# K/Q transposes and score masks of a recurrent attention step, issued as four 32-column TensorE tiles each

## The chip, the cores and the metric

The kernel runs on one core of a Trainium2 chip. The metric is the device time of one launch in microseconds, the median of several runs. A core has a matrix engine (TensorE, PE in the profile; its weight loads are listed apart as PEld), three engines for elementwise work (VectorE or DVE, ScalarE or ACT, GpSimd or POOL), and SyncE (SP), which issues most transfers. TensorE multiplies a stationary operand, loaded with a weight load, by a moving operand that is streamed through, and writes into PSUM, from where VectorE or ScalarE copies the result to SBUF. A weight operand of 32 columns can be given a place in the array, a tile of 32 of its 128 columns, named in the code by `tile_position=(0, 32*j)`; its result then lies in 32 of the 128 partitions of PSUM.

## What is computed

Four layers, A, B, A, B, each with a layer norm before it and a residual sum after it, over 2048 tokens of width 640. The change lies in layer B, a recurrence over 64 segments of 32 tokens with 8 rows of memory:

```python
def _B_ref(x, mem0, Wq, Wk, Wv, Wo, seg_len):
    B, S, Dm = x.shape
    H, Dh = (Wq.shape[1], Wq.shape[2])          # 32, 128
    M = mem0.shape[1]                           # 8
    scale = Dh ** (-0.5)
    n_seg = S // seg_len                        # 64
    L = M + seg_len                             # 40
    idx = jnp.arange(L)
    mask = (idx[:, None] < M) | (idx[:, None] >= idx[None, :])
    mem = mem0
    outs = []
    for s in range(n_seg):
        xs = x[:, s * seg_len:(s + 1) * seg_len, :].copy()
        h = jnp.concatenate([mem, xs], axis=1)
        q = jnp.einsum('btd,dhe->bhte', h, Wq)
        k = jnp.einsum('btd,dhe->bhte', h, Wk)
        v = jnp.einsum('btd,dhe->bhte', h, Wv)
        scores = jnp.einsum('bhqe,bhke->bhqk', q, k) * scale
        scores = jnp.where(mask[None, None], scores, -1000000000.0)
        p = _softmax(scores, axis=-1)
        o = jnp.einsum('bhqk,bhke->bhqe', p, v)
        o = jnp.einsum('bhte,hed->btd', o, Wo)
        mem = o[:, :M, :].copy()
        outs.append(o[:, M:, :])
    return jnp.concatenate(outs, axis=1)
```

The memory rows of one segment are outputs of the segment before it, so the 64 segments of a layer run one after another. Two layers B make 128 steps.

## The kernel before

`layer_B` runs a Python loop over the steps (line 854), which writes out one instruction stream per engine. The wrapper `_OrdNC` (line 115) ties each instruction of an engine to the one before it, so every engine runs its instructions in the order of the code; all of them carry line 105 in the profile, and they are told apart by the names of their tiles.

A step works on 32 columns: the 8 memory rows that the step before has just produced and the 24 token rows of the segment after (the last 8 token rows of each segment, the tails, are projected ahead in batches, and arrive through DRAM as `b_tl` for keys and queries and as `b_Vth` for values). In order:

- `thin_mm` (line 658) makes the projections Ka, Qa, Kb, Qb (lines 944 to 950), heads 0 to 15 in the a halves and 16 to 31 in the b halves. Each is 20 products of 128x32 weights (the columns `b_HX`) with 512 moving columns, in four tiles of 32 columns. Each result is copied to a tile `b_kq` by ScalarE (Ka, Kb, Qb) or VectorE (Qa).
- `transp4` (line 667) transposes each copy, with 4 transposes of 128x128, into PSUM: TPak, TPaq, TPbk, TPbq (lines 953 to 963). The copy is the stationary operand, the identity `C.identb` the moving one. TPbq has a PSUM tile of its own (tag "tail").
- After each, VectorE copies the 8 memory rows to `b_KT` or `b_QT` of this step (`scatter`, line 674), and ScalarE the 24 token rows to those of the next step (`x_scatter`, line 867).
- `mask_mm` (line 878) opens the score tiles SP0 (8 groups of 40 columns) and SP1 (4 groups) with the mask: one product of the identity with 320 columns of `mask12`, and one with 160. The first stands ahead of TPbq, the second behind it.
- `scores` (line 885) adds the products of queries and keys in tiles of 32 columns: 16 of heads 0 to 15 (`b_QT`), then 32 small ones with the tails' queries (`b_QZ`), all into SP0, then 16 of heads 16 to 31 into SP1. SP0 is thus complete after 48 of the 64.
- Softmax (lines 968 to 979): maximum over SP0, then over SP1, subtraction, exponential on ScalarE, sum, reciprocal, and the probabilities `b_Pm` and `b_Px`. Meanwhile TensorE makes the values Va and Vb (lines 983 and 985, in tiles as above), a part of the batch projections of tails (`tail_unit`, in 110 of the steps), and in some steps the transposes of the next layer-normed input (`ln_spread`, tile `b_lntps`).
- `p_transp` transposes the probabilities (PTP), `pv` multiplies them by the values (OTP), `o_mm` applies the output weights (OPS), and lines 1028 to 1043 bring the 8 new memory rows into the columns of the next step (`b_msb`, `b_MT`, `b_HX`), with which Ka of the next step begins.

The PSUM tiles of the pool "b_ps" (5 buffers) are taken in turn; SP1 follows Qb in its buffer, and Va follows TPak. What an engine waits for is settled by semaphores. One is raised at the last transpose of a set, one at the last of the 48 products into SP0, and one at the last of the 16 into SP1.

Of the kernel before, what the change touches and what calls it, by code (L numbers as in the profile page):

```python
# [542 lines left out]
def layer_B(nc, tc, C, W, x_src, xb_src, x_dst, mem0, B_Wv, B_Wo, nsteps=64, out_bf16=False, tag=""):  # L543
    SCB = 1.0 / math.sqrt(128.0)
    nc_raw = nc
    nc = _OrdNC(tc, nc_raw, engines=ORDER_ENGINES)
# [4 lines left out]
    with ExitStack() as ctx:  # L551
# [21 lines left out]
        def ps_tile(shape, dtype, name):  # L573
            return pp.tile(shape, dtype, name=name, tag="ps")
# [4 lines left out]
        mask12 = st.tile([128, 12, 40], BF16, name="b_mask12")  # L579
# [87 lines left out]
        def transp4(sb, name, tp=None):  # L667
            if tp is None:
                tp = ps_tile([128, 4, 128], BF16, name)
            for i in range(4):  # L670
                nc.tensor.transpose(tp[:, i, :], sb[:, 128 * i:128 * i + 128], C.identb[:])
            return tp

        def scatter(eng, tp, b, dst_t, t0, t1, c0):
# [107 lines left out]
        for nm, b in jobs:  # L782
            ps = thin_mm(cols, W.wk if nm == "K" else W.wq, b, f"b_{nm}p")
            sb = kqp.tile([128, 512], BF16, name="b_kq", tag="kq")
# [5 lines left out]
        for (nm, b), sb in zip(jobs, sbs):  # L790
            tp = transp4(sb, "b_TP")
            scatter("dve" if nm == "K" else "act", tp, b, KT[0] if nm == "K" else QT[0], 8, 32, 8 if nm == "K" else 0)
# [61 lines left out]
        for s in range(nsteps):  # L854
# [23 lines left out]
            def mask_mm(a):  # L878
                g0, g1 = GR[a]
                SP = ps_tile([128, g1 - g0, 40], F32, f"b_SP{a}")  # L880
                nc.tensor.matmul(SP[:].rearrange("p g k -> p (g k)"), lhsT=C.identb[:], rhs=mask12[:, g0:g1, :].rearrange("p g k -> p (g k)"),
                                 start=True, stop=False, skip_group_check=True)
                return SP

            def scores(SPs):
# [65 lines left out]
            qb = kq(Qb, "act", SCB)  # L951

            TPak = transp4(ka, "b_TPak")
            scatter("dve", TPak, 0, KT[s], 0, 8, 32)
            x_scatter(TPak, 0, KT)
            TPaq = transp4(qa, "b_TPaq")
            scatter("dve", TPaq, 0, QT[s], 0, 8, 24)
            x_scatter(TPaq, 0, QT)
            TPbk = transp4(kb, "b_TPbk")
            scatter("dve", TPbk, 1, KT[s], 0, 8, 32)  # L960
            x_scatter(TPbk, 1, KT)
            SPa = mask_mm(0)
            TPbq = transp4(qb, "b_TPbq", po.tile([128, 4, 128], BF16, name="b_TPbq", tag="tail"))
            scatter("dve", TPbq, 1, QT[s], 0, 8, 24)
            x_scatter(TPbq, 1, QT)
            SPb = mask_mm(1)
            scores((SPa, SPb))
            soft_max(0, SPa)
# [59 lines left out]
            if not last:  # L1028
# [5 lines left out]
                for pi, (ca, cb) in enumerate(parts):  # L1034
                    mt = ps_tile([128, cb - ca, 8], F32, f"b_MT{pi}")
                    for c in range(ca, cb):
                        for q in range(4):
                            o = 64 * c + 32 * (q % 2)
                            nc.tensor.matmul(mt[32 * q:32 * q + 32, c - ca, :], lhsT=msb[:, o:o + 32], rhs=selm[:, q // 2, :],
                                             start=True, stop=True, tile_position=(0, 32 * q), skip_group_check=True)  # L1040
# [107 lines left out]
```

## Time and profile before

| | |
|---|---|
| median of 3 runs | 2867.46 us (2866.17 to 2868.26) |
| the profiled execution | 2871.54 us, its span 2869.8 us |
| granted TensorE clock, mean | 0.975 |
| DMA | 156.40 MB, mean 54 GB/s |
| HBM read, written | 95.65 MB, 51.38 MB |
| layer B's steps in the span | from 461 to 1444 us and from 1880 to 2862 us, about |
| b_Ka, b_Qa, b_Kb, b_Qb, b_Va, b_Vb | 2520 products each, 379 to 381 ns each |
| b_TPak, b_TPaq, b_TPbk, b_TPbq | 512 transposes of 128x128 each, 219 to 222 ns each |
| b_SP<-b_mask | 128 products of 320 columns, 299 ns, and 128 of 160, 233 ns |
| b_SP<-b_KT | 4096 products with b_QT, 186 ns each, 4096 with b_QZ, 181 ns |
| VectorE's copies of the transposes (b_KT, b_QT) | 128 each of 223 to 226 ns |

The duration of a product runs from its start to the modelled end of its way through the array. Products overlap, so what a set costs is read from where the next set starts, not from the sum of the durations. "128*32 128x512" after a product's names is its stationary and its moving operand; "x20" means 20 of them in a row. In the timeline a number in brackets is the time for which the engine stood idle before the instruction, with the tile that it waited for.

### The profile page before, as it was taken

The page shows a single profiled execution, that of the slowest core. Times are in us where ns is not written, and L with a number is a line of the kernel's source. Part 1 is how long each engine was busy: PE and PEld are TensorE (multiplying, and loading weights), DVE is VectorE, ACT ScalarE, POOL GpSimd, SP SyncE. Part 2 cuts the span into 40 slices and gives each one's busy share as a digit, 9 for nine tenths or more (in the row PEclk, how much of TensorE's full clock was granted, in tenths as well). Part 3 has the DMA queues.
Part 4 walks back from the last instruction along what each step waited for, and adds up shares of the span by engine and source line. Part 5 has one row for each costly group of instructions (what it writes and reads, how often), then busy time and mean ns, then how long its engine had stood idle before and what let it go on. Part 6 is the DMA issues. An engine that isn't in the chain of part 4 may idle for free.

```text
span 2869.8 us, 145239 instructions
## 1 busy us (share of the span) xinstructions
PE 2671.2 (93%) x64776; PEld 1669.4 (58%) x64776; DVE 1646.2 (57%) x4428; ACT 1555.7 (54%) x3390; POOL 633.2 (22%) x1506
## 2 busy tenths in 40 slices
PE   5899998999999999999969999889999999999988
PEld 2455555666666666665535555556666666666655
DVE  5778854555555555544468878545555555555544
ACT  3777863545445455544438777544455455445533
POOL 3456551100000000000025666400000000010000
PEclk8999999999999999999989999999999999999999
DMA  5110144222221122111130111621111111111110
GB/s 212 53 43 28 33 142 118 44 43 43 44 43 42 42 46 43 40 40 29 23 120 20 57 47 35 198 71 40 42 39 38 43 41 41 42 39 38 38 22 19
DMA packets 322947, 156.40 MB, mean 54 GB/s; under 512 B 245776, under 2 KB 311056, under 8 KB 319248
## 3 DMA queue, kind: packets, MB, share of 16 engines
q1 hardware_dynamic: 320880, 136.63, 18.8%
q8 instruction: 506, 8.29, 1.2%
q10 hardware_dynamic: 1440, 10.49, 1.0%
q14 instruction: 121, 0.99, 0.1%
HBM read 95.65 MB, written 51.38 MB: 51 GB/s over the span
## 4 chain that ended last, share of the span: by engine, by line
PE 61%; DVE 13%; ACT 4%; DMA 3%; issue 2%; POOL 1%; SPq 0%; ACTq 0%; DVEq 0%; POOLq 0%
PE b_OPS L105 11%; PE b_Ka L105 6%; PE b_Qb L105 5%; PE b_Kb L105 5%; PE b_Qa L105 5%; PE b_SP L105 4%; PE b_OTP L105 3%; PE b_OPSd L105 3%; DVE b_ssum L105 3%; PE b_tail L105 2%; PE b_vtail L105 2%; DVE b_negmax L105 2%; PE b_PTP L105 2%; DVE b_SP L105 2%; ACT b_E L105 2%
## 5 line engine op out<-in xcount | busy, mean ns | idle before, releaser
L105 PEld LDWEIGHTS <-b_HX 128*32 128x32 bf16 x15360 | 412.1, 97 | 374.1 <-issue 16.5
L375 DVE TENSOR_REDUCE a_nm<-a_S 128x2 f32<-128x1024 f32 (+3 forms) x512 | 403.5, 811 | 92.3 <-PE a_T L407 70.8
L410 ACT ACTIVATE a_PT<-a_T 128x1024 bf16<-128x1024 f32 (+1 forms) x384 | 341.0, 892 | 51.9 <-PE a_T L407 46.7
L105 POOL COPY b_OTdef<-b_OTsb 128x256 bf16<-128x256 bf16 x128 | 51.2, 400 | 1360.0 <-DVE b_OTsb L105 1288.6
L105 PE MATMUL b_OPS<-b_wo,b_OTsb 128*32 128x320 bf16 x8192 | 327.0, 311 | 12.7 <-issue 7.6
L105 PEld LDWEIGHTS <-b_OTsb 128*32 128x32 bf16 x8192 | 217.0, 100 | 104.2 <-DVE b_OTsb L105 28.1
L412 POOL TENSOR_SCALAR_AFFINE_SELECT a_PT<-a_PT 128x256 bf16<-128x256 bf16 (+1 forms) x384 | 197.3, 516 | 235.6 <-ACT a_PT L410 234.4
L105 ACT CAST b_msb<-b_OPS 128x128 bf16<-128x128 f32 x252 | 61.5, 295 | 294.2 <-PE b_OPS L105 294.2
L105 DVE CAST b_HX<-b_MT 128x16 bf16<-128x16 f32 x248 | 44.2, 178 | 268.8 <-PE b_MT L105 257.5
L105 ACT CAST b_kq<-b_Kb 128x512 bf16<-128x512 f32 x128 | 74.9, 585 | 201.4 <-PE b_Kb L105 201.4
L105 DVE TENSOR_SCALAR b_kq<-b_Qa 128x512 bf16<-128x512 f32 x128 | 88.5, 692 | 157.3 <-PE b_Qa L105 157.2
L105 DVE CAST b_OTsb<-b_OTP 128x160 bf16<-128x160 f32 (+1 forms) x384 | 122.0, 373 | 90.5 <-PE b_OTP L105 90.4
L105 PE MATMUL b_Ka<-b_wk,b_HX 128*32 128x512 bf16 x2520 | 159.2, 381 | 6.0 <-DVE b_HX L105 0.3
L105 PE MATMUL b_Va<-b_wv,b_HX 128*32 128x512 bf16 x2520 | 161.0, 380 | 0.0
L105 PE MATMUL b_Vb<-b_wv,b_HX 128*32 128x512 bf16 x2520 | 160.3, 379 | 0.0
L407 PE MATMUL a_T<-a_q,a_kT 32*128 32x512 bf16 (+3 forms) x1024 | 139.5, 306 | 21.2 <-DVE a_nm L375 14.6
L105 DVE COPY b_KT<-b_TPak 128x128 bf16<-128x128 bf16 x128 | 28.7, 224 | 227.2 <-PE b_TPak L105 227.2
L105 PE MATMUL b_Qb<-b_wq,b_HX 128*32 128x512 bf16 x2520 | 157.9, 379 | 0.0
L105 PE MATMUL b_Qa<-b_wq,b_HX 128*32 128x512 bf16 x2520 | 157.8, 379 | 0.0
L105 PE MATMUL b_Kb<-b_wk,b_HX 128*32 128x512 bf16 x2520 | 157.8, 379 | 0.0
L105 PEld LDWEIGHTS <-b_kq 128*128 128x128 bf16 x2080 | 116.9, 98 | 69.9 <-ACT b_kq L105 55.6
L105 ACT CAST b_kq<-b_Ka 128x512 bf16<-128x512 f32 x128 | 74.9, 585 | 147.0 <-PE b_Ka L105 147.0
(196 smaller groups left out, 5586.7 us busy)
## 6 DMA issues: line engine op xcount, KB each, us to landing
b_QKd<-b_tu SPq DMA_DIRECT2D x128, 128.0 KB
b_tl<-b_QKd SPq DMA_DIRECT2D x128, 128.0 KB
b_wv<-in_B_Wv_dram SPq DMA_DIRECT2D x10, 1024.0 KB
b_wo<-in_B_Wo_dram SPq DMA_DIRECT2D x16, 640.0 KB
b_VTd<-b_vt SPq DMA_DIRECT2D x256, 32.0 KB
b_Vth<-b_VTd SPq DMA_DIRECT2D x512, 16.0 KB
b_XO<-xres SPq DMA_DIRECT2D x256, 30.0 KB
b_wk<-in_B_Wk_dram ACTq DMA_DIRECT2D x5, 1024.0 KB
```

Of the source, the lines that this page charges most:

```text
L105: r = f(*a, **k)
L375: nc.vector.tensor_reduce(out=nm[:, qc, 2 * pr:2 * pr + 2], in_=X[:, :, o:o + w_], axis=AX.X, op=ALU.max, negate=True)
L407: nc.tensor.matmul(Y[:, e, o:o + w_], lhsT=kT[rows, 128 * kc:128 * kc + 128], rhs=q2[rows, 128 * kc:512], start=True, stop=True, tile_posi ...
L410: nc.scalar.activation(out=PT[:, :, b:b + width], in_=Y[:, :, 0:width], func=ACT.Exp, scale=SC)
L412: nc.gpsimd.affine_select(out=dv, in_=dv, pattern=[[0, 2], [0, diag], [1, 128]], compare_op=ALU.is_ge, fill=0.0, base=0, channel_multiplie ...
```

## The change

Two places in layer B. `transp4` issues, for each of the 4 blocks of 128 columns, four transposes of 32 columns in the four column tiles in place of one of 128x128: 16 instructions for 4, with the same identity as the moving operand. `mask_mm` issues four products in the four column tiles in place of one: each takes 32 columns of the identity as its weights and the same mask columns as before. The results lie where they did. Order, semaphores, copies and transfers are as they were, but for the number of TensorE's instructions: 64 transposes and 8 mask products a step where there were 16 and 2. `transp4` is also called four times in the preamble of each layer B (line 791).

```diff
@@ -668,7 +668,9 @@
             if tp is None:
                 tp = ps_tile([128, 4, 128], BF16, name)
             for i in range(4):
-                nc.tensor.transpose(tp[:, i, :], sb[:, 128 * i:128 * i + 128], C.identb[:])
+                for q in range(4):
+                    o = 128 * i + 32 * q
+                    nc.tensor.transpose(tp[32 * q:32 * q + 32, i, :], sb[:, o:o + 32], C.identb[:], tile_position=(0, 32 * q))
             return tp
 
@@ -878,8 +880,10 @@
             def mask_mm(a):
                 g0, g1 = GR[a]
                 SP = ps_tile([128, g1 - g0, 40], F32, f"b_SP{a}")
-                nc.tensor.matmul(SP[:].rearrange("p g k -> p (g k)"), lhsT=C.identb[:], rhs=mask12[:, g0:g1, :].rearrange("p g k -> p (g k)"),
-                                 start=True, stop=False, skip_group_check=True)
+                for q in range(4):
+                    r = slice(32 * q, 32 * q + 32)
+                    nc.tensor.matmul(SP[r].rearrange("p g k -> p (g k)"), lhsT=C.identb[:, r], rhs=mask12[:, g0:g1, :].rearrange("p g k -> p (g k)"),
+                                     start=True, stop=False, tile_position=(0, 32 * q), skip_group_check=True)
                 return SP
```

## The prediction

> **What bounds the kernel now.** I read the page, then one recurrent step of layer B in the timeline, then the chain of waits through that step, and last the single starts of TensorE's instructions. The page says that TensorE is nearly always occupied and that its instructions are fetched in 506 pieces:
>
> ```profile
> PE 2671.2 (93%) x64776; PEld 1669.4 (58%) x64776; DVE 1646.2 (57%) x4428; ACT 1555.7 (54%) x3390; POOL 633.2 (22%) x1506
> ...
> q8 instruction: 506, 8.29, 1.2%
> ```
>
> 93% suggests that each nanosecond taken off TensorE counts. The timeline of one step (start, length, engine, what) says otherwise:
>
> ```profile
> 708.09 1.25 PE L105 MATMUL b_Qb<-b_wq,b_HX 128*32 128x512 bf16 x20
> ...
> 709.28 0.40 PE L105 MATMUL b_TPak<-c_identb,b_kq 128*128 128x128 bf16 x4
> 709.46 0.60 ACT L105 ACTIVATE b_kq<-b_Qb 128x512 bf16<-128x512 f32 x1 [0.50 <-PE b_Qb L105]
> 709.51 0.39 PE L105 MATMUL b_TPaq<-c_identb,b_kq 128*128 128x128 bf16 x4
> ...
> 709.74 0.39 PE L105 MATMUL b_TPbk<-c_identb,b_kq 128*128 128x128 bf16 x4
> ...
> 709.96 0.30 PE L105 MATMUL b_SP<-b_mask,c_identb 128*128 128x320 bf16 x1
> ...
> 710.11 0.40 PE L105 MATMUL b_TPbq<-c_identb,b_kq 128*128 128x128 bf16 x4
> ...
> 710.34 0.23 PE L105 MATMUL b_SP<-b_mask,c_identb 128*128 128x160 bf16 x1
> ...
> 710.51 0.28 PE L105 MATMUL b_SP<-b_KT,b_QT 128*32 128x40 bf16 x16
> 710.54 0.22 DVE L105 COPY b_QT<-b_TPbq 128x128 bf16<-128x128 bf16 x1 [0.16 <-PE b_TPbq L105]
> ...
> 710.62 0.41 PE L105 MATMUL b_SP<-b_KT,b_QZ 128*16 128x40 bf16 x32
> ...
> 710.86 0.32 PE L105 MATMUL b_SP<-b_KT,b_QT 128*32 128x40 bf16 x16
> ...
> 711.00 1.27 PE L105 MATMUL b_Va<-b_wv,b_HX 128*32 128x512 bf16 x20
> ...
> 711.15 0.72 DVE L105 TENSOR_REDUCE b_negmax<-b_SP 128x8 f32<-128x320 f32 x2 [0.39 <-PE b_SP L105]
> ```
>
> The reader is to see three things. First, the two changes of tile shape: Ka, Qa, Kb and Qb follow each other every 1.08 us (705.93, 707.01, 708.09), so the transposes could begin at 709.17 and begin at 709.28, 0.11 late; the small mask product (half of the 0.15 from 709.96 to 710.11, so done streaming at 710.41) is followed by scores at 710.51, 0.10 late. In the single starts the two gaps are 96 and 94 ns, in each of the 128 steps. Second, ScalarE's copy of Qb runs 709.46 to 710.06, and TPbq starts 0.05 behind it. Third, the row maximum on VectorE (b_negmax) starts right behind the scores. From there the chain of waits leaves TensorE until the probabilities are transposed:
>
> ```profile
> 710.51 0.62 PE b_SP L105 x49
> ...
> 711.15 0.55 DVE b_negmax L105 x2
> ...
> 713.85 0.26 DVE b_Pm L105
> 714.11 0.35 DVE b_Px L105
> ...
> 714.51 0.44 PE b_PTP L105 x6
> ```
>
> So a step is a loop of latencies: projections, Qb's copy, TPbq, scores, softmax, output, next memory rows. A step of this kind takes 14.97 us whether it carries tail work or not (starts of Ka 566.87, 581.84 here; 14.97 also for the shortest steps without tails), so TensorE's 93% isn't what sets it.
>
> **The change part by part**, against the profiled execution (span 2869.8 us, 2871.54 with what lies around it; 0.14% over the median of 2867.46, to which I apply the difference). There are 128 steps.
>
> *First shape change (0.10 us).* Removed; price nothing. TPak, TPaq, TPbk and the large mask product move 0.10 up, then TPbq stands waiting: it needs Qb's copy, which starts from Qb's end, not from the transposes. Cover: ScalarE's 0.60 us copy. Without it the gain were 128 x 0.10 = 12 us more.
>
> *Transposes.* A transpose of 128 moving columns starts every 56 ns now (709.28, 709.51, 709.74: four per 0.225). Four tiles of 32 output rows are to share that time. No column-tiled transpose is in the trace. Rows around it: projections with 512 columns give a group of four per 216 ns (1.08 / 5), the output product with 320 columns one per 136 ns, the scores with 40 columns one per 25 to 33 ns (64 pairs in 0.49 us). All but the last are the columns at 2.4 per ns plus 3, so 128 columns give 56 ns: a set of 16 takes 0.224 as now, plus up to 25 ns until the fourth tile of the last group starts. Bounds: 0 and, without overlap, 16 x 56 = 0.90 us (rival 3). I take 0.02 for TPbq: VectorE's copy of it (256 ns after the last start, 0.22 long) ends at 710.79 instead of 710.77, the second half of the scores may start 0.06 later at 710.85, and starts at 710.86 now. So V stays at 711.00: nothing gained, nothing lost there. The earlier x_scatter copies on ScalarE are queued behind Qb's copy and don't move.
>
> *Mask products.* 320 and 160 columns in four tiles at once: 133 and 67 ns as now.
>
> *Second shape change (0.094 us).* This one lies on the path: the first 48 score pairs (16 of heads 0-15, 32 with QZ) wait for nothing later than TPbk, so they start at 710.42 instead of 710.51. The maximum over SP0 waits for the last of these 48, not for the second half. They took 0.345 us, 33 pairs at 6.3 ns and then 8.3 ns a pair, the fastest that instructions go out anywhere here. Since 32 more instructions of TPbq go out just before, fewer are in hand: at 8.3 ns for all of them 48 take 0.40. Thus the gain is at least 0.094 - 0.055 = 0.03. At most it is 0.094 + 0.02 (all at 6.3) + 0.08, since the maximum starts 302 ns after the last of the 48 now, with TensorE issuing flat out behind it, where the copies of the transposes, 37 ns more of streaming taken off, start after 219. I take 0.12. Softmax then starts 0.12 earlier; PTP can follow, since the last tail product before it starts 180 ns ahead of it in a plain step.
>
> Not in all steps: in 24 of them the input transposes (b_lntps) and their two copies on ScalarE stand between V and PTa, and V doesn't move: price nothing. 104 x 0.12 = 12.5 us gained (bounds 3 and 21).
>
> *Added instructions.* Per step 48 transposes and 6 mask products, each with a weight load: 108 more, in all 13,824 and 192 in the two preambles. 8.29 MB for 129,552 instructions are 64 bytes each, a fetch of 16 KB is 256 of them: 55 fetches more. Their price shows where TensorE has no stock: here, in another step, 16 scores take 0.54 instead of 0.32 though nothing is waited for, and V and the maximum come 0.22 late:
>
> ```profile
> 587.86 0.54 PE L105 MATMUL b_SP<-b_KT,b_QT 128*32 128x40 bf16 x16
> ...
> 588.37 0.72 DVE L105 TENSOR_REDUCE b_negmax<-b_SP 128x8 f32<-128x320 f32 x2 [0.61 <-PE b_SP L105]
> ```
>
> Steps with tail work and without b_lntps take 15.21 us in the mean and 14.96 at least; put on 3.6 fetches a step, that is 68 ns a fetch: 55 x 0.068 = 3.7 us lost (bounds 0 and twice that).
>
> Sum: -12.5 + 3.7 = -8.8 us, 2862.7 for the profiled execution, **2859** for the median. By the bounds 2847 to 2872.
>
> **The rivals.**
> 1. *Nothing moves.* In the step just shown and wherever V is late, the maximum is late by as much, 0.16 behind V's first start, though it waits for an earlier product. If it is tied to the later starts, only the fetches remain: 2867.5 + 3.7 = 2871. Against it: the semaphore it waits for belongs to the 48.
> 2. *Slower: instruction supply becomes the bound between TPbq and V.* There 2 x (16 + 4 + 64) = 168 instructions would go out at the highest pace instead of 138 behind a full stock. A fetch's pause of 0.22 falls there in 168 / 256 of the steps, 0.144 a step, where now some 15 of 63 steps show 0.2, 0.05 a step: 104 x 0.094 = 9.8 lost; with the low gain (3) and the other fetches (3.7): 2878. It decides once pauses there cost more than the 0.12 gained, about 0.09 a step more than my 0.03.
> 3. *Slower: tiles of a transpose don't overlap.* Sets of 0.90: the fourth starts its last transpose at 712.83, the second half of the scores comes at 713.37 instead of 710.86, 128 x 2.5 = 320 us, 3187. It begins to lose when a group of four takes over 80 ns, 4 x 24 being the 94 ns gained. For it: transposes in tiles don't occur here. Against it: four other products do, and overlap. [...] By the scores of this trace, where four loads of 32 columns and four products pass in 25 to 33 ns, such loads aren't serial.
>
> **How the numbers follow.** No change means within 0.2% (5.7 us), what a measurement of this kernel can tell. Forecast 0.45 (of it 0.05 ends within 0.2%), rival 1 0.23 (0.03 of it slower), rival 2 0.22, rival 3 0.10. Faster 0.40, the same 0.25, slower 0.35. The range reaches from the forecast's lower bound, 2847, over rival 2 to 2888 (its pause at twice the price); rival 3 is left out.
>
> **What would show it.** Right: TPak 1.08 us behind Qb's first start; sets of transposes still 0.22 to 0.25; TPbq still 0.05 behind Qb's copy (first saving absorbed); scores 0.07 behind the small mask product; V still some 0.89 behind TPbq, b_negmax about 0.04 behind V's first start instead of 0.15; plain steps of 14.85 us. Wrong: a set of transposes over 0.32; b_negmax still 0.15 behind V; scores of 0.5 us in most steps; steps of 14.97.

## The result and the profile after

The changed kernel took 2888.59 us in the median of 5 runs (2881.15 to 2894.94). The kernel before took 2867.41 us beside it, also 5 runs (2866.17 to 2868.26). The ratio is 1.0068, with a 95% interval of 1.0045 to 1.0091. So it is slower, and 0.6 us past the upper end of the forecast range. The profiled execution of the changed kernel is the one of 2888.59 us, with a span of 2886.8 us, 17.0 us more than before.

The page of the changed kernel: TensorE's busy time fell by 5 us although it issues 14,016 instructions more (half of them, 7,008, in each of its two counts), and these came in 55 more pieces, as forecast:

```profile
PE 2666.5 (92%) x71784; PEld 1678.9 (58%) x71784; DVE 1646.1 (57%) x4428; ACT 1560.9 (54%) x3390; POOL 635.6 (22%) x1506
...
q8 instruction: 561, 9.19, 1.4%
```

The timeline of a step of the changed kernel in which nothing goes wrong (start, length, engine, what; Ka starts at 960.01):

```profile
963.26 1.25 PE L105 MATMUL b_Qb<-b_wq,b_HX 128*32 128x512 bf16 x20
964.34 0.40 PE L105 MATMUL b_TPak<-c_identb,b_kq 128*32 128x128 bf16 x16
964.56 0.40 PE L105 MATMUL b_TPaq<-c_identb,b_kq 128*32 128x128 bf16 x16
964.62 0.60 ACT L105 ACTIVATE b_kq<-b_Qb 128x512 bf16<-128x512 f32 x1 [0.50 <-PE b_Qb L105]
...
965.01 0.31 PE L105 MATMUL b_SP<-b_mask,c_identb 128*32 128x320 bf16 x4
...
965.27 0.41 PE L105 MATMUL b_TPbq<-c_identb,b_kq 128*32 128x128 bf16 x16
...
965.51 0.24 PE L105 MATMUL b_SP<-b_mask,c_identb 128*32 128x160 bf16 x4
965.58 0.27 PE L105 MATMUL b_SP<-b_KT,b_QT 128*32 128x40 bf16 x16
965.68 0.43 PE L105 MATMUL b_SP<-b_KT,b_QZ 128*16 128x40 bf16 x32
...
966.01 0.28 PE L105 MATMUL b_SP<-b_KT,b_QT 128*32 128x40 bf16 x16
966.13 1.25 PE L105 MATMUL b_Va<-b_wv,b_HX 128*32 128x512 bf16 x20
966.23 0.72 DVE L105 TENSOR_REDUCE b_negmax<-b_SP 128x8 f32<-128x320 f32 x2 [0.27 <-PE b_SP L105]
```

TPak now starts 1.08 us behind Qb, so the first gap is gone. TPbq stands 0.05 behind the end of Qb's copy (964.62 + 0.60), as before: the first saving went into that wait. The scores start 0.07 behind the small mask product, not 0.17. The maximum starts 0.10 behind V's first start, and V itself is now 6.12 behind Ka. The next step begins at 974.89, after 14.88 us.

The chain of waits through the same step passes through the same work as before:

```profile
965.32 0.36 PE b_TPbq L105 x16
965.68 0.52 PE b_SP L105 x52
...
966.23 0.55 DVE b_negmax L105 x2
...
968.93 0.26 DVE b_Pm L105
969.19 0.35 DVE b_Px L105
...
969.58 0.45 PE b_PTP L105 x6
```

So the undisturbed step did get shorter. The very next one, the timeline of the changed kernel from 980 us on, shows where the time was lost:

```profile
980.89 0.28 PE L105 MATMUL b_SP<-b_KT,b_QT 128*32 128x40 bf16 x16
...
981.00 0.38 PE L105 MATMUL b_Va<-b_wv,b_HX 128*32 128x512 bf16 x2
981.11 0.72 DVE L105 TENSOR_REDUCE b_negmax<-b_SP 128x8 f32<-128x320 f32 x2 [0.27 <-PE b_SP L105]
...
982.16 1.26 PE L105 MATMUL b_Va<-b_wv,b_HX 128*32 128x512 bf16 x18 [0.77 <-issue]
982.16 1.84 PEld L105 LDWEIGHTS <-b_HX 128*32 128x32 bf16 x37 [1.08 <-issue]
...
985.17 0.24 PE L105 MATMUL b_PTP<-c_identb,b_Pm 128*128 128x128 bf16 x2
...
990.82 1.26 PE L105 MATMUL b_Ka<-b_wk,b_HX 128*32 128x512 bf16 x20
```

TensorE stops after two products of Va for 1.08 us and waits for "issue": no engine, no buffer, no transfer that the profile knows. The maximum is not delayed (981.11 is 6.22 after Ka, as in the step above). But TensorE runs its instructions in the order of the code: V, the tail products and PTP all come 1.05 later (PTP 10.28 after Ka instead of 9.23), and the step ends at 990.82, 15.93 after its Ka. The whole pause reached the end of the step.

The view of waits (in total us, times, longest us) of the kernel before, and then of the changed kernel:

```profile
PEld L105 <- issue: 92.3, 185, 7.0
PE b_OPS L105 <- issue: 7.6, 17, 1.0
```

```profile
PEld L105 <- issue: 145.2, 283, 6.8
PE b_OPS L105 <- issue: 13.2, 28, 1.1
PE b_Va L105 <- issue: 5.9, 13, 0.9
PE b_Vb L105 <- issue: 4.8, 12, 0.6
```

The weight loads of layer B wait for their own issue 283 times instead of 185, and waits in Va and Vb are in the list for the first time. Not all of the 52.9 us is on the path, so I took the price from the steps. The starts of the first b_Ka give the length of each step. "Plain" is with tail work and without b_lntps; the first and last step of each layer are left out; ns, shortest / mean:

| kernel | TensorE instructions in a plain step | 84 plain | 24 with b_lntps | 16 without tails |
|---|---|---|---|---|
| before | 868 | 14964 / 15208 | 15174 / 15356 | 14966 / 16164 |
| after | 976 | 14875 / 15439 | 15117 / 15640 | 14854 / 15239 |

The shortest plain step fell by 89 ns, but its distance to the mean rose from 0.244 to 0.564 us (with b_lntps from 0.182 to 0.523). Thus the 17 us of the profiled execution are: 84 x 0.089 + 24 x 0.057 = 8.9 gained on the path, 84 x 0.320 + 24 x 0.341 = 35 lost in pauses, 14.8 gained in the 16 steps without tails (see under "Not foreseen" below), and 1.7 + 3.9 lost in first steps and outside layer B's steps.

The trace also says what the pauses are. In layer B's steps TensorE stands idle for over 0.15 us with nothing but "issue" to wait for 70 times, 30.0 us in all, where the kernel before has 19 such waits and 8.0 us. From one of the 70 to the next it is always a whole number of pieces, that is of 128 pairs of load and product, but for at most 4 pairs, and each of them ends 1.2 to 1.7 us after the latest fetch of a piece has landed. In the step above a piece begins with the first transposes at 979.34; its 128 pairs have gone out by 981.01; the next piece had landed at 980.73, and TensorE goes on at 982.16.

### The profile page after: what moved, and what is told of

Read it like the earlier page. It is cut to its first block, busy times and chain, and to the rows that moved or that the text cites. A ratio compares the mean times of both kernels' runs of the same rounds, so it can differ in the third digit from the quotient of the medians.

```text
span 2886.8 us, 159257 instructions
## 1 busy us (share of the span) xinstructions
PE 2666.5 (92%) x71784; PEld 1678.9 (58%) x71784; DVE 1646.1 (57%) x4428; ACT 1560.9 (54%) x3390; POOL 635.6 (22%) x1506
## 3 DMA queue, kind: packets, MB, share of 16 engines
q8 instruction: 561, 9.19, 1.4%
## 4 chain that ended last, share of the span: by engine, by line
PE 64%; DVE 10%; ACT 4%; issue 3%; DMA 2%; POOL 1%; SPq 1%; ACTq 0%; POOLq 0%; DVEq 0%
PE b_OPS L105 10%; PE b_Ka L105 6%; PE b_Qb L105 5%; PE b_Qa L105 5%; PE b_Kb L105 5%; PE b_tail L105 3%; PE b_SP L105 3%; PE b_OTP L105 3%; PE b_Va L105 3%; PE b_OPSd L105 3%; PE b_Vb L105 2%; PE b_vtail L105 2%; DVE b_ssum L105 2%; PE b_PTP L105 2%; DVE a_nm L375 2%
## 5 line engine op out<-in xcount | busy, mean ns | idle before, releaser
L105 PEld LDWEIGHTS <-b_HX 128*32 128x32 bf16 x15360 | 400.8, 96 | 408.0 <-issue 43.2
L105 PE MATMUL b_OPS<-b_wo,b_OTsb 128*32 128x320 bf16 x8192 | 321.0, 304 | 18.9 <-issue 13.2
L105 PE MATMUL b_Vb<-b_wv,b_HX 128*32 128x512 bf16 x2520 | 167.9, 379 | 5.0 <-issue 4.8
L105 PEld LDWEIGHTS <-b_kq 128*32 128x32 bf16 x8320 | 130.8, 97 | 57.1 <-ACT b_kq L105 26.3
L407 PE MATMUL a_T<-a_q,a_kT 32*128 32x512 bf16 (+3 forms) x1024 | 140.2, 308 | 23.0 <-DVE a_nm L375 16.5
```

What stands on the lines that cost most here:

```text
L105: r = f(*a, **k)
L407: nc.tensor.matmul(Y[:, e, o:o + w_], lhsT=kT[rows, 128 * kc:128 * kc + 128], rhs=q2[rows, 128 * kc:512], start=True, stop=True, tile_posi ...
```

## The experiments

The theory is that TensorE runs out of instructions. The page of the changed kernel has 9.19 MB in 561 fetches for TensorE's 2 x 71,784 instructions: a piece of 16 KB holds 256, so 128 pairs of load and product. In the kernel before, the stretch from TPak to the last score holds 164 instructions, in the changed one 272, in about the same 1.8 us. The rivals: one part of the change costs time by itself (a shape, a set), the places where the pieces end matter and not their density, or something else in the step is later.

**One part at a time.** Three kernels take a part of the change each; `transp4` and `mask_mm` got a switch for it, for late_pair:

```diff
+                if not tiled:
+                    nc.tensor.transpose(tp[:, i, :], sb[:, 128 * i:128 * i + 128], C.identb[:])
+                    continue
...
+            MASK_TILED = (1,)
...
+                if a not in MASK_TILED:
+                    nc.tensor.matmul(SP[:].rearrange("p g k -> p (g k)"), lhsT=C.identb[:], rhs=mask12[:, g0:g1, :].rearrange("p g k -> p (g k)"),
+                                     start=True, stop=False, skip_group_check=True)
+                    return SP
...
-            TPbq = transp4(qb, "b_TPbq", po.tile([128, 4, 128], BF16, name="b_TPbq", tag="tail"))
+            TPbq = transp4(qb, "b_TPbq", po.tile([128, 4, 128], BF16, name="b_TPbq", tag="tail"), tiled=True)
```

In early_three it is `tiled=True` at TPak, TPaq and TPbk with `MASK_TILED = (0,)`, in masks_only `MASK_TILED = (0, 1)` alone.

late_pair:

> TPbq and the small mask product in tiles, all else as before: 30 TensorE instructions more a step (898 in a step with tail work) in place of 108. The change of tile shape moves ahead of TPbq, where TensorE waits for Qb's copy anyway. Supply theory (a piece of 256 TensorE instructions can't be had oftener than every 3.3 to 3.9 us, so the 108 were too many): shortest steps 14.88 as in the changed kernel, pauses nearly as in the kernel before, 2855 to 2866 us. Tile theory (column tiles of transposes disturb what follows, whatever the count): the pauses of the changed kernel in the measure of the tiled sets, 2870 or more.

early_three:

> The other part alone: TPak, TPaq, TPbk and the large mask product in tiles, TPbq and the small mask product as before: 78 TensorE instructions more a step (946). The shape change ahead of the scores stays, so nothing is gained on the path. Supply theory: shortest steps 14.97, pauses between those of the two kernels, 2878 to 2895 us. Were it shape changes alone: 2867, no change.

masks_only:

> Only the mask products in tiles: 12 TensorE instructions more a step, and two shape changes more ahead of TPbq. If a shape change costs 0.095 us wherever it lies on the path: TPbq starts 0.17 later (5.26 + 0.17 after Ka), V too, 128 x 0.17 = 22 us, 2889. If the gap ahead of the scores belongs to the scores and not to the shape: 2867 to 2870.

Beside a median of 2866.37 before: late_pair 2882.57, ratio 1.0047 (1.003 to 1.0064), a miss; early_three 2875.79, 1.0033 (1.0017 to 1.005), a little below its expectation; masks_only 2899.92, 1.0107 (1.009 to 1.0124), slower than expected. The timeline of late_pair (Ka at 692.93):

```profile
698.04 0.30 PE L105 MATMUL b_SP<-b_mask,c_identb 128*128 128x320 bf16 x1
698.27 0.41 PE L105 MATMUL b_TPbq<-c_identb,b_kq 128*32 128x128 bf16 x16
698.50 0.24 PE L105 MATMUL b_SP<-b_mask,c_identb 128*32 128x160 bf16 x4
698.57 0.27 PE L105 MATMUL b_SP<-b_KT,b_QT 128*32 128x40 bf16 x16
```

TPbq starts 5.34 after Ka instead of 5.26. The large mask product streams for 0.136, the pace of the output products with as many columns, and a shape change adds 0.095 behind it (0.23 from its start to TPbq's, 0.15 before), so the shape change moved from in front of the scores to in front of TPbq, where it ends later than Qb's copy. The shortest plain step (14.953) is 0.011 shorter than before, not 0.09. In masks_only the shape changes four times (Ka at 724.74):

```profile
729.63 0.39 PE L105 MATMUL b_TPbk<-c_identb,b_kq 128*128 128x128 bf16 x4
729.95 0.32 PE L105 MATMUL b_SP<-b_mask,c_identb 128*32 128x320 bf16 x4
730.20 0.40 PE L105 MATMUL b_TPbq<-c_identb,b_kq 128*128 128x128 bf16 x4
730.53 0.25 PE L105 MATMUL b_SP<-b_mask,c_identb 128*32 128x160 bf16 x4
```

TPbk to mask is 0.32 instead of 0.22, TPbq to mask 0.33 instead of 0.23, and the shortest plain step is 15.173, 0.209 more than before. So a shape change costs some 0.095 us each, and costs it in the end where it lies on the path; this also makes the gain of the full change real. early_three leaves the shortest step where it was (14.967): the early shape change alone is worth nothing, as forecast. But its pauses did not rise, though the supply theory had expected it: as in the kernel before, there are 8.0 us of waits of over 0.15 us (18 of them), with 78 more instructions in a step and 242 in the dense stretch.

late_pair's loss is not explained by its steps in layer B: in its profile they sum to 1935.4 us, before to 1934.5. The difference of its execution lies mostly in code of layer A that nobody changed, 456.9 us between the two layers' steps instead of 451.1, of which 61.4 at half the granted clock instead of 51.2. Why the clock was halved there more often stays open; before_shift, below, has the same, 454.7 us with 58.0 of them at half the clock.

**Fewer and more instructions.** cut_before and cut_after take a part of the tail work out of the kernel before and the changed one, which removes 64 TensorE instructions from a plain step:

```diff
@@ tail_unit
-                for c in range(NCH):
+                for c in range(1):
                     nc.tensor.matmul(ps[:, i, :], lhsT=Wt[:, c, 128 * h:128 * h + 128], rhs=TX[T][:, c, :, :].rearrange("p s t -> p (s t)"),
-                                     start=(c == 0), stop=(c == NCH - 1))
+                                     start=True, stop=True)
```

cut_before:

> The kernel before with the batch projection of the tails' keys and queries cut to the first of its five chunks of 128 features: 64 TensorE instructions less in a step with tail work (804), 0.93 us of TensorE's time less off the path. Supply theory: the pauses shrink, 2840 to 2862 us. Tile theory: as before but for the freed time, 2855 to 2867.

cut_after:

> The changed kernel with the same cut (912 instructions in a step with tail work). Supply theory: most of the pauses go, and the 0.09 us a step gained on the path shows: 5 to 12 us faster than the cut kernel before. Tile theory: still some 15 to 25 us slower than the cut kernel before.

Beside 2867.64 before: cut_before 2870.17, ratio 1.0007 (0.9986 to 1.0028), slower than both theories had expected; cut_after 2853.75, 0.9944 (0.9924 to 0.9964), 16.4 us faster than cut_before, more than expected. The times mix two things. One is the granted clock: its mean over the executions was 0.975 in the kernel before, 0.967 in cut_before and 0.971 in cut_after, and cut_before's own executions took from 2860.41 us at 0.970 to 2882.74 at 0.960. By that slope, an estimate, some 10 of the 16.4 us go with the clock, and the two profiled executions, both at 0.968, took 2864.0 and 2863.9. The other is the pauses. The waits of cut_before, and then of cut_after, columns as above:

```profile
PE b_OPS L105 <- issue: 4.3, 8, 1.1
```

```profile
PE b_OPS L105 <- issue: 5.7, 13, 0.9
PE b_Vb L105 <- issue: 2.5, 6, 0.8
```

The waits of over 0.15 us at the ends of pieces came to 5.1 us instead of 8.0 in the kernel before, and to 15.2 instead of 30.0 in the changed one. The plain steps that kept the whole clock (75 and 77 of them) have their mean 0.187 and 0.251 us over the shortest instead of 0.244 and 0.564. So with 64 instructions less in a plain step, and the tiles as they were, about half of the pauses went, not most of them.

Then cut_before was filled up to the changed kernel's count of instructions without any tile in the transposes. 86 tiny products (54 without tails) go ahead of Va, into the PSUM that Va overwrites:

```diff
-        def thin_mm(cols_ap, Wt, b, name):
+        def thin_mm(cols_ap, Wt, b, name, extra=0):
...
+            for x in range(extra):
+                j = x % 4
+                nc.tensor.matmul(ps[32 * j:32 * j + 32, 0:8], lhsT=cols_ap[:, 0, :], rhs=Wt[:, 0, 0:8],
+                                 start=True, stop=True, tile_position=(0, 32 * j), skip_group_check=True)
...
-            Va = thin_mm(cols, W.wv, 0, "b_Va")
+            Va = thin_mm(cols, W.wv, 0, "b_Va", extra=86 if unit else 54)
```

cut_before_pad300 has `extra=300` in every step, cut_before_pad_split `extra=43 if unit else 27` at Va and again at Vb.

cut_before_pad:

> The cut kernel before, with small products of 8 columns ahead of Va that Va overwrites: 86 in a step with tail work, 54 in the others, so that the number of TensorE instructions is the changed kernel's (976 and 856) while no transpose or mask is in tiles. They take about 0.7 us of TensorE while softmax runs, less than the 0.93 that the cut freed. Supply theory: 20 to 40 us slower than the cut kernel before. Tile theory: as the cut kernel before, within 5 us.

cut_before_pad300:

> The same with 300 such products in every step (1404 TensorE instructions, 1348 in steps without tail work). By their pace of 8.3 ns they take 2.5 us, 1.5 to 2.4 beyond what is covered: steps of 16.5 to 17.4 us, 3060 to 3180 in all. Supply theory: 5.5 pieces at 3.3 to 3.9 us, steps of 18 to 21.4 us, 3260 to 3700, and starts of fetches at one even distance, which is the time that a piece costs.

cut_before_pad_split:

> The padded kernel again with the same number of small products, half ahead of Va and half ahead of Vb. If the number in a step alone decided, as slow as the padded kernel (2991). If what decides is whether 256 instructions in a row pass in less than a fetch's 3.3 to 3.9 us, thinning them out helps: 2880 to 2950.

cut_before_pad took 2990.82 us, ratio 1.0433 (1.0388 to 1.0478): 120.7 us over cut_before, far more than expected. The shortest plain step is unchanged (14.968 against 14.965), so in a plain step the products themselves are free; the mean is 16.34. The waits of cut_before_pad, columns as above:

```profile
PE b_Va L105 <- issue: 60.5, 38, 2.4
...
PE b_OPS L105 <- issue: 25.3, 27, 1.9
```

cut_before_pad_split issues the same 976 in a step, and took 2938.52, ratio 1.027 (1.0251 to 1.0289), some 60% of the loss (the two ran on different chips). Its largest wait moved to where its second half is:

```profile
PE b_Vb L105 <- issue: 54.8, 54, 1.5
```

Thus it isn't the count in a step alone, which is equal in after and both of these, with excess over the kernel each was made from of 0.7%, 4.2% and 2.4%. It is also how many come in a row with little work each. cut_before_pad300 (3952.03, ratio 1.3778, 1.3707 to 1.3848) is beyond even the 3700 that the supply theory allowed; its granted clock was 0.869 in the mean, and how much of the excess is the clock's was not separated. It shows the mechanism bare, in the timeline of one step:

```profile
678.34 0.35 PE L105 MATMUL b_SP<-b_KT,b_QT 128*32 128x40 bf16 x16
678.51 1.13 PE L105 MATMUL b_Va<-b_wv,b_HX 128*32 128x8 bf16 x106
681.99 1.18 PE L105 MATMUL b_Va<-b_wv,b_HX 128*32 128x8 bf16 x128 [2.35 <-issue]
685.46 2.83 PE L105 MATMUL b_Va<-b_wv,b_HX 128*32 128x8 bf16 x86 [2.30 <-issue]
```

128 pairs, which are one piece, run in 1.18 us; then TensorE waits 2.3 us. The piece that begins at 681.99 and the next, at 685.46, are 3.47 us apart. In the 131 places of this kernel where two pieces follow like that, 3.46 to 4.03 us pass, 3.75 in the median: that is the pace of supply for each 256 instructions when TensorE has nothing in hand. In layer B of before, after, after_again and this kernel the starts of two fetches are never less than 3.2 us apart. The changed kernel's 976 instructions in 14.88 us are 3.81 pieces, 3.9 us each: close to the limit, and its 272 in 1.8 us are far over it, so they live from what is in hand. How much TensorE can have in hand was not shown.

**Only where the supply is not strained.** In tiles_no_tail the 18 steps without tail work have the change, the other 110 have not: `tiled=not unit`, and the plain mask product `if unit`.

> The change only in the 18 steps without tail work, where a step has 748 TensorE instructions (856 with the tiles), the other 110 as before. Supply theory: no pauses added, 18 x 0.09 = 1.6 us gained on the path; if the half-clock stretches of those steps become fewer, up to 15 us more: 2850 to 2867. Tile theory: pauses in those steps as in the changed kernel's others, 2868 to 2875.

The kernel took 2857.83, ratio 0.9995 (0.9981 to 1.0009). Its changed steps have a shortest of 14.850 instead of 14.966, the others stay at 14.965. Eighteen steps at 0.1 us are 2 us, too few to show. It is the best form found, and no faster than the kernel before beyond its interval.

**The same kernel again, and moved pieces.** after_again and after_third are the changed kernel as it is, on two chips. before_shift and after_shift have 64 transposes of the identity more at the start of layer A, where TensorE waits for its input (2.91 us ahead of the first transposes in the kernel before); after that every piece begins 128 instructions earlier.

```diff
+            if not SHIFTED:
+                SHIFTED.append(1)
+                for x in range(64):
+                    nc.tensor.transpose(tps[:, x % 5, :], C.identb[:], C.identb[:])
             for c in range(NCH):
                 nc.tensor.transpose(tps[:, c, :], xn[:, 128 * c:128 * c + 128], C.identb[:])
```

after_again:

> The changed kernel once more, beside the other two: 2880 to 2895 us. Its profile tells whether the stretches at half clock in layer B (37.5 us of the span in the kernel before, 13.7 in the changed one) are fewer again: then it is the change, otherwise chance.

before_shift:

> The kernel before with 64 extra transposes of the identity (128 instructions, half a piece of 256) ahead of the first transposes of layer A, where TensorE waits for the input anyway; their result is overwritten. Every piece of instructions then begins 128 instructions earlier in all later code, and nothing else differs. Supply theory (pauses depend on how dense 256 instructions in a row are issued, and where the boundaries fall only redistributes them): within 0.25% of before, ratio 0.9975 to 1.0025. Rival (placement: the changed kernel lost mainly because its boundaries fell on worse places of the step and of layer A): this shift alone moves the time by more than 0.3% either way.

after_shift:

> The changed kernel with the same 64 extra transposes at the start. Supply theory: slower than before by the same as without the shift, ratio 1.003 to 1.008 (1.0068 and 1.0032 were measured on two chips), about 25 us of pauses in layer B's steps in the profile. Rival (placement): ratio moves by more than 0.4% from these, to 1.000 or below or over 1.011.

after_third:

> The changed kernel as it is, beside its shifted form on the same chip. Both theories: ratio 1.003 to 1.008; it is the base for the shifted form.

after_again took 2869.80, faster than expected, with 2862.38 for the kernel before beside it, ratio 1.0032 (1.0017 to 1.0047). The last three ran beside 2866.55: before_shift 2872.29, 1.0028 (1.0011 to 1.0045); after_shift 2884.73, 1.0062 (1.0049 to 1.0076); after_third 2895.34, 1.0101 (1.0086 to 1.0116), over its expectation.

| ns over the shortest step, mean | plain | with b_lntps | all 126 steps, us |
|---|---|---|---|
| before | 244 | 182 | 1934.5 |
| before_shift | 295 | 185 | 1935.0 |
| after | 564 | 523 | 1947.6 |
| after_third | 554 | 464 | 1947.2 |
| after_shift | 486 | 511 | 1945.2 |
| after_again | 374 | 353 | 1928.2 |

The shift alone costs the kernel before 0.28%, a bit more than the supply theory allowed and a bit less than its rival asked for, and takes 0.4% off the changed kernel. The first of these goes with the granted clock: before_shift's executions had 0.967 to 0.975 of it, the slowest two, of 2886.93 and 2887.51 us, had the 0.967, and where the clock was 0.974 or 0.975 they took 2864.95 to 2873.50, the kernel before 2865.41 to 2871.47. Whether the shift or chance lowered the clock isn't shown. At the same clock of 0.974 or 0.975 the changed kernel took 2894.08 (after_third, one execution) and 2879.66 and 2886.93 (after_shift, two), so its loss is not the clock's. The placement of the pieces is not the cause either: with either placement the changed kernel has 1.6 to 2.9 times the pauses of the kernel before, and over both of them on this chip it is some 0.7% slower ((1.0062 + 1.0101) / 2 against (1 + 1.0028) / 2). The chip may have a part too: after_again and after_third are one program, but a fetch's packet took 1.07 us in the mean in the first and 1.13 in the second, and their pauses come to 15 and 33 us more than in the profile of before (35 in after, where the packet took 1.15; 28 in after_shift). Two chips don't show that the packet is the reason. The loss was 0.3 to 1.0% in all four.

With 0.3% between placements, the parts' ratios of 1.0033 and 1.0047 can't be told from a change of placement or of clock. For early_three and late_pair only the step lengths and the pauses are evidence; where late_pair's loss comes from stays open.

## Why the prediction was wrong

- *What bounds the kernel*: right. The step is a loop of latencies; undisturbed steps followed the terms below.
- *First shape change, price nothing*: right. The gap went from 96 to -10 ns, and TPbq starts 5.262 after Ka instead of 5.264.
- *Transposes, a set in 0.224 us and 0.02 for TPbq*: right. The sets start 0.22 apart, and VectorE's copy of TPbq ends 0.022 later. "V stays at 711.00" was a little off: V starts 0.036 earlier, since the second half of the scores came 0.013 earlier and went out faster, with no price in the sum. Rival 3, tiles that don't overlap, is out: the 16 weight loads of a set add nothing to its 0.22 us.
- *Second shape change, 0.12 us on the path, bounds 0.03 to 0.20*: right in kind, the size is 0.091 for the maximum and 0.089 for the plain step. The maximum starts 0.10 behind V and not 0.04, since V moved too; its distance from the last of the 48 pairs stayed at 0.30, where the 0.12 had counted on some of that going away. So 104 x 0.12 = 12.5 should have been 104 x 0.089 = 9.3. The steps with b_lntps, priced at nothing, gained 0.057 each. All of this holds for undisturbed steps: in 52 of the 84 plain steps the maximum came over 0.01 us later than in those (before: 29). Rival 1 is out.
- *Added instructions, 55 x 0.068 = 3.7 us, bounds 0 and twice that*: **this is the step that failed.** The count of fetches was exact. The price was not: pauses rose by 35 us in the profiled execution (15 to 35 over four profiles), 4 to 9 times the term. It took the pauses of the kernel before, spread over all its fetches, as the price of one more fetch. Most fetches come without a long wait: in the 126 steps 420 of them with 19 waits of over 0.15 us before, and 473 with 70 after, of up to 1.1 us each (2.4 in cut_before_pad). The added ones all lie in one dense stretch of 1.8 us, and the price did not go up evenly with them: with 78 of the 108 a step (early_three, 242 instructions in the stretch, less than a piece) the long waits stayed at 8.0 us, with all of them (272, more than a piece) they came to 30.0. That the stretch must hold a whole piece is a reading of these kernels, not a test.
- *Rival 2, the instruction supply becomes the bound, 2878*: the right mechanism, at chance 0.22. Its place was off: it looked for pauses between TPbq and V of 0.22 us, but the stock mostly lasts through the scores and runs out behind them, in Va and Vb, and later in OPS, for up to 1.1 us. There it holds V, tail work and PTP, in the step shown without touching the maximum. "Its pause at twice the price" gave the upper end of 2888, which was just passed; that it came so near is chance, since the gain of 14.8 us below stands in no term.
- *Slips in the sums*: 0.094 - 0.055 is 0.04 and not 0.03; 48 pairs at 6.3 ns take 0.30 us, 0.04 less than 0.345 and not 0.02; a step has 3.3 fetches and not 3.6 (420 in 126 steps); V is late in 15 of 63 steps, but by 0.2 us in 5 of them and by 0.035 in the mean, not 0.05. None of them moves a term or a bound by more than about 2 us.
- *Not foreseen*: 14.8 us gained in the 16 steps without tails, which the prediction had no term for. In the view by stretches (us, then busy time and count of each engine, granted clock, DMA share, GB/s) the kernel before while it applies the output weights in one such step, and then the changed kernel at that place of the same step:

```profile
1312.20:1315.50 3.30, 3.30 (x54) 1.99 (x56) 1.45 (x4) 0.38 (x2) 1.21 (x4) 0.50 0.09 23
```

```profile
1326.20:1329.50 3.30, 2.83 (x92) 1.80 (x83) 1.62 (x6) 0.62 (x3) 1.22 (x4) 1.00 0.13 22
```

The granted clock is halved for stretches of 3.41 us in steps without tails: in layer B's 126 steps 37.5 us in all before, 10.2 after (13.7 with the one in a layer's last step), 10.2 in after_again. Eleven of the 16 steps took 16.5 to 16.9 us before, three after and three in after_again. But in cut_before and before_shift, where these steps are the same as before, it was six and eight, and in after_shift and after_third five, so a part of this gain is chance of the two profiled executions. Without it the profiled execution would have lost 17.0 + 14.8 = 32 us. Why fewer steps meet it was not settled; from the start of the last product of Vb to that of PTP it is 1.17 us in most of these steps instead of 1.20.

## What to carry to other kernels

Count TensorE's instructions, weight loads included, in every dense stretch, and hold them against the supply measured in cut_before_pad300, 256 per 3.46 to 4.03 us; splitting a product into four tiles multiplies its instructions by four, and what it saves in shape changes (0.095 us each, and only those on the path) can be less than what the empty queue costs: here 8.9 us against 35. An average pause per fetch in a kernel that is seldom short of instructions is no price for one that often is (here 0.068 us a fetch against 35 / 55, some 0.64): look at how long the stock lasts behind the densest stretch, and at what is queued in order behind it. Where two kernels differ by only 0.3%, compare executions at the same granted clock and put a shifted form beside them before a part is blamed.

## What the hardware showed unexpectedly

- In cut_before_pad300 TensorE took 256 instructions in 1.18 us, but with nothing in hand a new piece came only every 3.46 to 4.03 us; the packet of a fetch itself took 1.07 to 1.15 us in the mean (after_again, after).
- A change of tile shape cost 0.094 to 0.096 us from the end of the old shape's streaming in the kernel before; in masks_only, where it happens twice more, the shortest step is 0.209 us longer.
- A wait of TensorE for its instructions ends 1.2 to 1.7 us after the piece has landed, in all 70 cases of the changed kernel.
- A shift of all code by 128 instructions went with a lower granted clock in the kernel before (0.972 in the mean instead of 0.975) and a time 0.28% longer; before_shift's 12 runs also spread wider, over 2864.95 to 2887.51, against 2856.26 to 2871.47 in 17 runs of the kernel before on the same chip.
- Half the clock was granted for 3.41 us in 11 of 16 steps of the kernel before that are nearly the same as the 5 others, which kept all of it.
